# Attention and a top-1 expert layer: logits before rows in each chunk, and another order of the work behind attention

## The chip, the core and the metric

One core of a Trainium2 chip runs the whole program. Its engines are TensorE (PE, matrix products into PSUM banks), VectorE (DVE), ScalarE (ACT), GpSimd (POOL) and SyncE (SP, which here only starts transfers); each takes its instructions in the order of the program and waits at semaphores. The metric is the device time of one execution in microseconds (us), the median over several runs.

## The reference

Sliding-window attention with a distance bias, and a layer of eight experts of which each token takes one:

```python
def _attn_ref(q, k, v):                       # 8 batches, 8 heads, 576 tokens, 64 wide
    scores = scale * np.matmul(q, k.transpose(0, 1, 3, 2))
    mask = (rel >= 0) & (rel < window)        # window 128
    scores = np.where(mask, scores + bias[None], -1000000000.0)
    attn = np.exp(scores - np.max(scores, axis=-1, keepdims=True))
    attn = attn / (np.sum(attn, axis=-1, keepdims=True) + 1e-09)
    return np.matmul(attn, v)

def _moe_ref(x, w_gate, w1, w2):              # x: 4608 tokens x 512; 8 experts, 1024 wide
    logits = x @ w_gate
    expert_idx = np.argmax(logits, axis=1)
    ...
    gate_w = probs[np.arange(N), expert_idx]
    for e in range(E):
        mask = expert_idx == e
        h = np.maximum(x[mask] @ w1[e], 0.0)
        out[mask] = gate_w[mask, None] * (h @ w2[e])
```

## The kernel before, in words

**Attention** takes 36 chunks of 128 tokens in an order that is written by hand: four steps for a chunk, and the table `LAGS` says in which step each part of a chunk stands (scores L138, mask L152 and maximum L155, exponentials L159, transposes L168, products with v L196, `rows`). `rows` ends a chunk: one product (L206) turns the chunk's result and forms its gate logits, into `r_ps`; then DVE multiplies by the reciprocal row sum in two instructions, E (the 16 gate columns of each of 4 pairs of heads) and D (the 128 result columns of each pair), both at L211. `done` (L1079) sums the gate columns into logits (lg, L1085) and lets SP store the rows to memory (`xd`, L1092).

**Routing** goes by groups of chunks (`GROUPS`). `route` is a generator in stages: one-hot (oh, L413) | rank product on PE (L419 to L423), pick, gates and their store (L494), run, t | p, lp, c | eq (L456), rr (L460) | index product ip (L466) and base (L468). A stage is issued at every fourth step. In most stages the small products of PE go into spare columns of `r_ps`, the bank that `rows` has last filled. The last full group is (30, 5), chunks 30 to 34; its last three stages stand in `route_last`, which routes chunk 35 alone (one-hot l_oh L515, rank L519, four l_lp L540, index products L543, idx L545).

**Early slices.** While routing ends, PE already runs the first expert's first layer for 256 tokens that were routed long before: seven slices of 12 products of 128x256 (L634, into the banks of `s_ps`), each followed by e_hh on ACT (L636) and e_hl on DVE (L637). A slice uses the bank of the last but one, so it waits for that slice's e_hl. `EP` and `LE` set where the slices stand.

**Experts.** `moe_static` begins with the second layer of these seven slices for two tiles (L762, `y_ps`, 42 products); between them stand the transposes of the rows of the next tokens (L596), which POOL gathers from memory (L587) once idx is there and the last rows and gates are stored. Ahead of the gathers POOL clears three pairs of buffers (hh and hl, L781). From then on PE works through eight experts.

The functions that the change touches, and what calls them:

Of the kernel before, what the change touches and what calls it, by code (L numbers as in the profile page):

```python
# [22 lines left out]
QB = 32  # L23
NP = H // 2
# [12 lines left out]
def attention(ctx, tc, st, qT, kT, v, c1, cb, iw, load_c2, chunk_done, chunks, begun):  # L37
# [163 lines left out]
    def rows(ch, subs, xT, rsum):  # L201
        rinv = small.tile([128, H], F32, name="rinv")
        nc.vector.reciprocal(out=rinv, in_=rsum)
        st["r_ps"] = r_ps = ps_r.tile([128, NP, 256], F32, name="r_ps")
        for p in range(NP):
            nc.tensor.matmul(out=r_ps[:, p, 0:XW], lhsT=xT[:, p, :], rhs=iw_sb[:, p, :], start=True, stop=True)  # L206
        x_sb = xp.tile([128, NP, XW], F32, name="x_sb")
        for lo, n in ((128, E), (0, D)):
            cols = slice(lo, lo + 2 * n)
            split = lambda ap: ap[:, :, cols].rearrange("q p (c x) -> q p c x", c=2)  # L210
            nc.vector.tensor_tensor(  # L211
                out=split(x_sb), in0=split(r_ps),
                in1=rinv.rearrange("q (p c) -> q p c", c=2).unsqueeze(3).to_broadcast([128, NP, 2, n]), op=ALU.mult)
        chunk_done(ch, subs, x_sb)

    ahead = {}
    done_q, done_v, scaled = {(0, 0), (0, 1), (0, 2)}, {(0, 0), (0, 1)}, {(0, 0)}
# [75 lines left out]

# [37 lines left out]
QA = 4  # L331
KA = 16
RB = 2
LW = (0, 0, 0, 0)
FREE_T = 146
WU = (9, 1, 1, 1, 1, 1, 2, 2, 2, 2, 2, 1, 0)
PACE = {21: (122, 126, 130, 132, 134), 27: (138, 142, 144, 146, 148), 30: (149, 150)}
# [1 line left out]
EARLY = 256  # L339
LATE = 27  # L340
NE = 7
EP = {60: "z", 134: "g", 143: "p0", 146: "p1", 147: "0", 149: "1", 150: "2"}
LE = ("3", "4", "56", "")
PF = (2, 3, 4)
BY_PARTS = 2
MAXOV = N // 128 + E
# [46 lines left out]
def route(tc, st, lg, c0, G, groups):  # L393
# [29 lines left out]
        nc.tensor.matmul(out=rank[:, E * g:], lhsT=tri[:, 1, :], rhs=f2(oh[:, 0:G - g]), start=False, stop=g == G - 1)  # L423
    pick = rp.tile(sh3, F32, name="pick")
    nc.vector.tensor_tensor(out=pick, in0=rank.rearrange("p (g e) -> p g e", e=E), in1=oh, op=ALU.mult)
    gate = rp.tile([128, G], F32, name="gate")
    nc.vector.tensor_reduce(out=gate, in_=ex, axis=AX.X, op=ALU.add)
    put_gates(tc, st, gate, groups)
    new = run[:, c0 + G, :]
    nc.vector.tensor_reduce(out=new, in_=oh.rearrange("p g e -> p e g"), axis=AX.X, op=ALU.add)  # L430
    nc.vector.tensor_tensor(out=new, in0=new, in1=run[:, c0, :], op=ALU.add)
    s = st["rank"][:, c0:c0 + G]
    nc.vector.tensor_reduce(out=s, in_=pick, axis=AX.X, op=ALU.add)
    t = rp.tile([128, G], F32, name="t")
    nc.vector.tensor_scalar(out=t, in0=s, scalar1=1.0 / 128, scalar2=-63.5 / 128, op0=ALU.mult, op1=ALU.add)
    nc.vector.tensor_scalar(out=t, in0=t, scalar1=12582912.0, scalar2=-12582912.0, op0=ALU.add, op1=ALU.add)
    if c0 + G == LATE:
        cnt = rp.tile([128, E], BF16, name="s_cnt")
        nc.vector.tensor_copy(out=cnt, in_=new)
# [17 lines left out]
                            in1=c.unsqueeze(2).to_broadcast(sc3), op=ALU.is_equal)  # L457
    rr = rp.tile([128, G, 2, E * TT], BF16, name="rr")
    for k, n in enumerate(("tokh", "tokl")):
        nc.vector.tensor_tensor(out=rr[:, :, k, :], in0=eq,  # L460
                                in1=st[n][:, c0:c0 + G].unsqueeze(2).to_broadcast(sc3), op=ALU.mult)
    yield
    ip = spare(st, 1, E * TT)
# [33 lines left out]
def route_last(tc, st, lg, ch, groups):  # L497
    nc = tc.nc
    rp = st["rp"]
    run = st["run"]  # L500
    tri = st["tri"]
    prev = rp.tile([128, E], BF16, name="l_prev", bufs=1)
    nc.vector.tensor_copy(out=prev, in_=run[:, ch, :])
    mx = rp.tile([128, 2], F32, name="l_mx", bufs=1)
    nc.vector.tensor_reduce(out=mx[:, 0:1], in_=lg, axis=AX.X, op=ALU.max)
    key = rp.tile([128, E], F32, name="l_key", bufs=1)
    nc.vector.scalar_tensor_tensor(out=key, in0=lg, scalar=mx[:, 0:1], in1=st["rev"], op0=ALU.is_ge, op1=ALU.mult)
    nc.vector.tensor_scalar(out=mx[:, 1:2], in0=mx[:, 0:1], scalar1=-1.0, scalar2=None, op0=ALU.mult)
# [12 lines left out]
    for r in st["rest"]:
        next(r)
        next(r)
    st["warm"](1)
    rr = rp.tile([128, 2, E], BF16, name="l_rr", bufs=1)
    for k, n in enumerate(("tokh", "tokl")):
        nc.vector.tensor_scalar(out=rr[:, k, :], in0=oh, scalar1=st[n][:, ch:ch + 1], scalar2=None, op0=ALU.mult)
    pick = rp.tile([128, E], F32, name="l_pick", bufs=1)
    s = st["rank"][:, ch:ch + 1]
    nc.vector.tensor_tensor_reduce(out=pick, in0=rank, in1=oh, op0=ALU.mult, op1=ALU.add, scale=1.0, scalar=0.0,  # L530
                                   accum_out=s)
    put_gates(tc, st, gate, groups)
    st["warm"](2)
    for r in st["rest"]:
        list(r)
    ip = st["ps_x"].tile([128, 512], F32, name="x_ps")[:, 0:E * TT]
    t0 = EARLY // 128
    for t in range(t0, TT):
        lp = rp.tile([128, 128], BF16, name=f"l_lp{t}", bufs=1)
        nc.vector.tensor_scalar(out=lp, in0=st["i128"], scalar1=s, scalar2=-128.0 * t, op0=ALU.subtract,  # L540
                                op1=ALU.is_equal)
        for k in range(2):
            nc.tensor.matmul(out=ip[:, E * t:E * t + E], lhsT=lp, rhs=rr[:, k, :], start=(k == 0), stop=(k == 1))  # L543
# [7 lines left out]
    st["warm"](3)  # L551


def slots(tc, st, pool, e, s0):
# [123 lines left out]
def moe_static(ctx, tc, st, w12, out):  # L678
# [7 lines left out]
    yp = ctx.enter_context(tc.tile_pool(name="m_y", bufs=YB))  # L686
    ps_l = ctx.enter_context(tc.tile_pool(name="ps_l", bufs=2, space=PSUM))
    ps_e = ctx.enter_context(tc.tile_pool(name="ps_e", bufs=1, space=PSUM))
    ps_y = [ctx.enter_context(tc.tile_pool(name=f"ps_y{n}", bufs=1, space=PSUM)) for n in (0, 2)]
    xs = {}  # L690
    xg = {}
    ys = {}
# [365 lines left out]
@with_exitstack  # L1058
def attn_moe_kernel(ctx, tc, qT, kT, v, c1, cb, c2, iw, w12, out):
    nc = tc.nc  # L1060
    st = {"stages": []}
    moe_pools(ctx, tc, st)
    load_c2 = load_consts(tc, st, c2)
    moe_early(ctx, tc, st)
# [4 lines left out]
    with ExitStack() as actx:  # L1069
# [9 lines left out]
        def done(ch, subs, x_sb):  # L1079
# [4 lines left out]
            lg = lgs["lg"]  # L1084
            nc.vector.tensor_reduce(out=lg[:, g, :], in_=x_sb[:, :, 128:XW].rearrange("q p (c e) -> q e p c", c=2),  # L1085
                                    axis=AX.XY, op=ALU.add)
            for lo in (0, 2):
                if lo == 2 and subs[0][0] == subs[2][0]:
                    continue
                n = 64 if subs[0][0] != subs[2][0] else 128  # L1090
                t0 = subs[lo][0] * S + QB * subs[lo][1]
                nc.sync.dma_start(out=st["xd"][t0:t0 + n].rearrange("t (p x) -> t p x", p=NP),  # L1092
                                  in_=x_sb[QB * lo:QB * lo + n, :, 0:SUB])
# [67 lines left out]
```

## Time and profile before

| | |
|---|---|
| median of three runs | 673.66 us (673.47, 673.66, 675.84) |
| profiled execution, its own time | 674.61 us |
| its span | 672.8 us |
| mean granted TensorE clock in it | 0.996 |
| busy in the span | PE 647.7, DVE 398.6, ACT 313.1, POOL 309.2 us |

The span is the part of the profiled execution between its first and its last instruction; 1.8 us of its time lie outside. Attention takes roughly the first 235 us, the passage to the experts the stretch up to 262 us, the experts the rest. A busy share says how long an engine had work, not whether it set the time; that is read from which engine stood idle for which.

### The profile page before, as it was taken

How to read it: one execution, taken by the hardware profiler on the slowest of the kernel's cores; microseconds unless marked ns; L12 is line 12 of the kernel's file. 1: busy time of each engine (PE TensorE's matmuls, PEld its weight loads, DVE VectorE, ACT ScalarE, POOL GpSimd, SP SyncE). 2: the span in 40 equal slices, each digit the busy share in tenths (PEclk: the TensorE clock that was granted, in tenths of full speed). 3: DMA queues.
4: the chain of work that ended last, by engine and by line, in shares of the span. 5: the costliest groups of instructions: out<-in, count | busy, mean ns of one | idle time of the engine just before them, and what ended most of it. 6: DMA issues, size and time to landing. Idle time of an engine off the chain costs nothing.

```text
span 672.8 us, 15622 instructions
## 1 busy us (share of the span) xinstructions
PE 647.7 (96%) x5937; PEld 551.2 (82%) x5937; DVE 398.6 (59%) x976; ACT 313.1 (47%) x940; POOL 309.2 (46%) x425
## 2 busy tenths in 40 slices
PE   7899999999999989999999999999999999999995
PEld 3688787787787878999988988989898989888884
DVE  3468878877888777553555355365456455456411
ACT  3777778887776511442234234233434333333311
POOL 2546567786654413016524751860762560471202
PEclk8999999999999999999999999999999999999999
DMA  9477696795853316335323442532543542453201
GB/s 319 131 199 182 177 248 164 256 261 133 264 144 82 94 34 189 111 117 170 93 81 109 144 128 82 181 106 85 173 107 109 174 114 77 159 147 111 89 0 59
DMA packets 55360, 94.24 MB, mean 140 GB/s; under 512 B 11622, under 2 KB 31334, under 8 KB 54386
## 3 DMA queue, kind: packets, MB, share of 16 engines
q1 hardware_dynamic: 46882, 73.18, 37.2%
q0 software_dynamic: 8400, 20.02, 10.4%
q8 instruction: 48, 0.79, 0.5%
q14 instruction: 30, 0.25, 0.1%
HBM read 74.20 MB, written 18.97 MB: 138 GB/s over the span
## 4 chain that ended last, share of the span: by engine, by line
PE 51%; issue 8%; POOL 3%; DMA 1%; DVE 1%; ACT 1%; POOLq 0%; ACTq 0%
PE y_ps L762 24%; PE l_ps L634 23%; POOL xg L614 2%; POOL out L749 1%; PE x_ps L762 1%; PE s_ps L634 1%; PE x_ps L596 1%; DMA xd<-x_sb 1%; PE x_ps L196 1%; DMA xg<-xd,idx 0%; PE r_ps L206 0%; DMA out<-y,od_pidx 0%; DVE x_sb L211 0%; ACT pe L159 0%; POOLq L812 0%
## 5 line engine op out<-in xcount | busy, mean ns | idle before, releaser
L637 DVE SCALAR_TENSOR_TENSOR hl<-l_ps,hh 128x334 fp32r<-128x334 f32 (+7 forms) x104 | 52.7, 506 | 162.5 <-ACT hh L636 162.4
L636 ACT ACTIVATE hh<-l_ps 128x334 fp32r<-128x334 f32 (+7 forms) x104 | 46.9, 451 | 216.4 <-PE l_ps L634 216.1
L614 POOL DMA_INDIRECT xg<-xd,od_idx x112 | 114.8, 1025 | 35.8 <-issue 35.2
L159 ACT ACTIVATE pe<-s_ps,nmax 128x128 f32<-128x128 f32 x288 | 102.2, 371 | 48.9 <-DVE nmax L155 39.8
L762 PE MATMUL y_ps<-wh,hh 128*128 128x512 f32 (+2 forms) x288 | 114.2, 397 | 0.0
L762 PE MATMUL y_ps<-wl,hh 128*128 128x512 f32 (+2 forms) x288 | 113.6, 394 | 0.0
L762 PE MATMUL y_ps<-wh,hl 128*128 128x512 f32 (+2 forms) x288 | 113.5, 394 | 0.0
L749 POOL DMA_INDIRECT out<-y,od_pidx x34 | 36.3, 1068 | 153.7 <-ACT y L768 147.2
L852 DVE TENSOR_TENSOR wl<-w_raw,wh 128x512 fp32r<-128x512 f32 x114 | 73.9, 689 | 23.2 <-ACT wh L848 22.1
L634 PE MATMUL l_ps<-xh,wl 128*128 128x304 f32 (+9 forms) x416 | 80.8, 316 | 0.0
L634 PE MATMUL l_ps<-xh,wh 128*128 128x304 f32 (+9 forms) x416 | 80.7, 316 | 0.0
L634 PE MATMUL l_ps<-xl,wh 128*128 128x304 f32 (+9 forms) x416 | 80.6, 316 | 0.0
L634 PEld LDWEIGHTS l_ps<-xh,wh 128*128 128x128 f32 x416 | 68.3, 189 | 7.4
L634 PEld LDWEIGHTS l_ps<-xh,wl 128*128 128x128 f32 x416 | 66.1, 189 | 2.0
L634 PEld LDWEIGHTS l_ps<-xl,wh 128*128 128x128 f32 x416 | 66.0, 189 | 1.9
L196 PE MATMUL x_ps<-pT,v_sb 128*64 128x128 f32 (+2 forms) x1152 | 66.4, 265 | 0.1
L762 PEld LDWEIGHTS y_ps<-wh,hl 128*128 128x128 f32 (+2 forms) x288 | 53.0, 184 | 13.9
L196 PEld LDWEIGHTS x_ps<-pT,v_sb 128*64 128x64 f32 (+1 forms) x1152 | 57.0, 137 | 7.8 <-issue 2.8
L762 PEld LDWEIGHTS y_ps<-wl,hh 128*128 128x128 f32 (+2 forms) x288 | 53.1, 184 | 11.6
L762 PEld LDWEIGHTS y_ps<-wh,hh 128*128 128x128 f32 (+2 forms) x288 | 53.0, 184 | 10.8 <-ACT hh L636 0.4
L159 ACT ACTIVATION_READ_ACCUMULATOR pe<-s_ps,nmax 128x1 f32 x288 | 60.2, 209 | 0.0
L138 PE MATMUL s_ps<-k_sb,q_sb 64*64 64x192 f32 (+2 forms) x1152 | 57.3, 307 | 2.6 <-DMA k_sb<-kT 2.6
(207 smaller groups left out, 980.6 us busy)
## 6 DMA issues: line engine op xcount, KB each, us to landing
w_raw<-w SPq DMA_DIRECT2D x64, 512.0 KB, 3.7
q_sb<-qT SPq DMA_DIRECT2D x40, 256.0 KB, 7.1
xd<-x_sb SPq DMA_DIRECT2D x32, 258.0 KB, 4.9
v_sb<-v SPq DMA_DIRECT2D x32, 256.0 KB, 4.9
k_sb<-kT SPq DMA_DIRECT2D x7, 1152.0 KB, 8.3
xg<-xd,od_idx POOLq DMA_INDIRECT x112, 3.2
xd<-x_sb SPq DMA_DIRECT2D x8, 129.0 KB, 4.2
v_sb<-v SPq DMA_DIRECT2D x8, 128.0 KB, 4.7
```

What stands on the lines that cost most here:

```text
L138: nc.tensor.matmul(out=s_ps[halves(a), c, n, x0:x1], lhsT=blocks["q", b, m][h, 2 * g + n, qs], rhs=batch[b][h, 2 * g + n, k0:k0 + x1 - x0] ...
L159: nc.scalar.activation(out=pe[:, h, :], in_=s_ps[:, c, n, lo:lo + 128], func=AF.Exp, bias=nmax[:, 2 * c + n:2 * c + n + 1], scale=1.0, acc ...
L196: nc.tensor.matmul(out=x_ps[64 * c:64 * c + 64, p, q], lhsT=blocks["v", b, m - 1 + kb][0:kk, D * h:D * h + D], rhs=pT[0:kk, kb, h, q], sta ...
L596: nc.tensor.transpose(out=x_ps[:, d, :], in_=g[:, SUB * d:SUB * d + 128], identity=st["ident"])
L614: ins = tc.nc.gpsimd.indirect_dma_start(out=g[:, s], out_offset=None, in_=parts, in_offset=bass.IndirectOffsetOnAxis(ap=idx[:, s], axis=0),)
L634: nc.tensor.matmul(out=ps, lhsT=a[:, 128 * d:128 * d + 128], rhs=b[:, d], start=(k == 0), stop=(k == 11))
L636: nc.scalar.activation(out=hh, in_=ps, func=AF.Relu)
L637: nc.vector.scalar_tensor_tensor(out=hl, in0=ps, scalar=0.0, in1=hh.bitcast(F32), op0=ALU.max, op1=ALU.subtract)
L749: ins = nc.gpsimd.indirect_dma_start(**kw).ins
L762: nc.tensor.matmul(out=ys[t][0:m], lhsT=a[:, tl], rhs=b[:, 512:1024], start=(f == 0 and k == 0), stop=(f == 7 and k == 2))
L852: keep(tc, eng.tensor_tensor(out=wl[:, sl], in0=raw[:, sl], in1=wh.bitcast(F32)[:, sl], op=ALU.subtract))
```

## The change

In `rows` only E stands right behind the product now; lg follows, and D and the store of the rows are put on a list (`st["later"]`) that is emptied at the end of the step, in `route_last` behind the rank products of chunk 35. In `route`, rank and t come ahead of run and the gates. The two rr of group (30, 5) go to POOL. The second early slice stands with the first ahead of that group's rank; in `route_last` the stages p to rr of that group stand ahead of slices 3 and 4, and the four l_lp ahead of the gates. The banks of the first tiles' second layer are swapped, so that `y_ps` no longer takes a bank on which base (before L468) is read.

```diff
+        def scale(lo, n):
...
+        scale(128, E)
+        chunk_done(ch, subs, x_sb, lambda: scale(0, D))
...
+        while st["later"]:
+            st["later"].pop(0)()
         if s in EP:
             early(EP[s])
...
-LW = (0, 0, 0, 0)
+LW = (0, 0)
...
-EP = {60: "z", 134: "g", 143: "p0", 146: "p1", 147: "0", 149: "1", 150: "2"}
-LE = ("3", "4", "56", "")
+EP = {60: "z", 134: "g", 143: "p0", 146: "p1", 147: "0", 149: "12"}
+LE = ("34", "56")
...
-        nc.vector.tensor_tensor(out=rr[:, :, k, :], in0=eq,
+        eng = nc.gpsimd if c0 + G == N // 128 - 1 else nc.vector
+        eng.tensor_tensor(out=rr[:, :, k, :], in0=eq,
...
     nc.vector.tensor_scalar(out=oh, in0=key, scalar1=mk, scalar2=None, op0=ALU.is_equal)
+    for r in st["rest"]:
+        next(r)
+        next(r)
     st["warm"](0)
...
-    for r in st["rest"]:
-        next(r)
-        next(r)
-    st["warm"](1)
+    while st["later"]:
+        st["later"].pop(0)()
...
-    ps_y = [ctx.enter_context(tc.tile_pool(name=f"ps_y{n}", bufs=1, space=PSUM)) for n in (0, 2)]
+    ps_y = [ctx.enter_context(tc.tile_pool(name=f"ps_y{n}", bufs=1, space=PSUM)) for n in (2, 0)][::-1]
...
-            for lo in (0, 2):
...
+            def store():
+                scale()
+                for lo in (0, 2):
...
+            st["later"].append(store)
```

Three places show the order. First DVE at the end of one chunk in attention, before and after (E is 128x4x16, D is 128x4x128):

```order
L203 RECIPROCAL rinv<-rsum 128x8
L211 TENSOR_TENSOR x_sb<-r_ps,rinv 128x4x16
L211 TENSOR_TENSOR x_sb<-r_ps,rinv 128x4x128
L1085 TENSOR_REDUCE lg<-x_sb 128x8
L152 COPY_PREDICATED s_ps<-c_sb,s_ps 128x4x128
```

```order
L203 RECIPROCAL rinv<-rsum 128x8
L212 TENSOR_TENSOR x_sb<-r_ps,rinv 128x4x16
L1093 TENSOR_REDUCE lg<-x_sb 128x8
L212 TENSOR_TENSOR x_sb<-r_ps,rinv 128x4x128
L152 COPY_PREDICATED s_ps<-c_sb,s_ps 128x4x128
```

lg has moved ahead of D, and nothing else.

Then DVE behind attention, from the one-hot of chunk 35 on (p to rr are group (30, 5), names with l_ are chunk 35), before and after:

```order
L515 TENSOR_SCALAR l_oh<-l_key,mk 128x8
L1031 MEMSET ov_cum 128x1
L637 SCALAR_TENSOR_TENSOR e_hl<-s_ps,e_hh 128x256
L444 SCALAR_TENSOR_TENSOR p<-t,rank 128x5
L446 TENSOR_TENSOR lp<-c_sb,p 128x640
L449 TENSOR_SCALAR c<-mk 128x5
L451 TENSOR_SCALAR big<-rank 128x5
L453 TENSOR_TENSOR c<-c,t 128x5
L454 TENSOR_TENSOR c<-c,big 128x5
L456 TENSOR_TENSOR eq<-c_sb,c 128x240
L460 TENSOR_TENSOR rr<-eq,c_sb 128x5x48 x2
L637 SCALAR_TENSOR_TENSOR e_hl<-s_ps,e_hh 128x256
```

```order
L521 TENSOR_SCALAR l_oh<-l_key,mk 128x8
L449 SCALAR_TENSOR_TENSOR p<-t,rank 128x5
L1039 MEMSET ov_cum 128x1
L451 TENSOR_TENSOR lp<-c_sb,p 128x640
L454 TENSOR_SCALAR c<-mk 128x5
L456 TENSOR_SCALAR big<-rank 128x5
L458 TENSOR_TENSOR c<-c,t 128x5
L459 TENSOR_TENSOR c<-c,big 128x5
L461 TENSOR_TENSOR eq<-c_sb,c 128x240
L645 SCALAR_TENSOR_TENSOR e_hl<-s_ps,e_hh 128x256 x2
L212 TENSOR_TENSOR x_sb<-r_ps,rinv 128x4x128
L534 TENSOR_SCALAR l_rr<-l_oh,c_sb 128x8 x2
```

The e_hl of slice 3 has moved behind eq, rr has left, and D of chunk 35 has come to stand behind two e_hl.

Last PE behind attention, from the end of group (30, 5)'s rank to the rank of chunk 35, before and after (the L634 or L642 rows are early slices, 12 products each):

```order
L423 MATMUL t_ps<-oh,tri 128x8
L634 MATMUL s_ps<-e_xh,wh 128x256 x4
L634 MATMUL s_ps<-e_xh,wl 128x256 x4
L634 MATMUL s_ps<-e_xl,wh 128x256 x4
L206 MATMUL r_ps<-iw_sb,xT 128x144 x4
L634 MATMUL s_ps<-e_xh,wh 128x256 x4
L634 MATMUL s_ps<-e_xh,wl 128x256 x4
L634 MATMUL s_ps<-e_xl,wh 128x256 x4
L519 LDWEIGHTS tri
L519 MATMUL x_ps<-l_oh,tri 128x8
L520 LDWEIGHTS tri
L520 MATMUL x_ps<-l_prev,tri 128x8
```

```order
L428 MATMUL t_ps<-oh,tri 128x8
L206 MATMUL r_ps<-iw_sb,xT 128x144 x4
L642 MATMUL s_ps<-e_xh,wh 128x256 x4
L642 MATMUL s_ps<-e_xh,wl 128x256 x4
L642 MATMUL s_ps<-e_xl,wh 128x256 x4
L642 MATMUL s_ps<-e_xh,wh 128x256 x4
L642 MATMUL s_ps<-e_xh,wl 128x256 x4
L642 MATMUL s_ps<-e_xl,wh 128x256 x4
L528 LDWEIGHTS tri
L528 MATMUL x_ps<-l_oh,tri 128x8
L529 LDWEIGHTS tri
L529 MATMUL x_ps<-l_prev,tri 128x8
```

Slice 2 has gone ahead of the rank (it stood first here before), and slice 4 has come ahead of the rank of chunk 35. Further on, 23 instead of 18 products of the second layer stand ahead of the first transposes of gathered rows, and all eight L543 products stand ahead of the first `y_ps` product, where they stood between such products.

## Rows read from the trace of the kernel before

**Rows 1.** The first part of the page (busy time, share of the span and number of instructions of each engine), and from its second part the granted TensorE clock in 40 slices of 16.8 us, in tenths of full speed (9 is 0.9 or more).

```profile
PE 647.7 (96%) x5937; PEld 551.2 (82%) x5937; DVE 398.6 (59%) x976; ACT 313.1 (47%) x940; POOL 309.2 (46%) x425
...
PEclk8999999999999999999999999999999999999999
```

**Rows 2.** The view of waits for TensorE (PE), 30 to 225 us of the span (the steady part of attention): what an instruction waited for, us in total, times, longest us.

```profile
PE t_ps L168 <- ACT pT L170: 4.3, 9, 0.7
PE r_ps L466 <- DVE x_sb L211: 3.1, 4, 1.2
```

**Rows 3.** The same view for VectorE (DVE), same stretch.

```profile
DVE s_ps L152 <- PE s_ps L138: 24.0, 28, 2.0
```

**Rows 4.** The view of waits for TensorE, 234 to 256 us (the passage from attention to the expert layers), same columns.

```profile
PE y_ps L762 <- DVE base L468: 0.9, 1, 0.9
PE t_ps L419 <- DVE oh L413: 0.8, 1, 0.8
PE x_ps L519 <- DVE l_oh L515: 0.6, 1, 0.6
PE s_ps L634 <- DVE e_hl L637: 0.6, 1, 0.6
```

**Rows 5.** The view of stretches: window in us: its length, then busy us (and instructions) of PE, PE weight load, DVE, ACT, POOL, then the granted TensorE clock (1 is full), DMA share, GB/s.

```profile
8.00:10.00 2.00, 1.75 (x26) 0.74 (x30) 1.06 (x2) 0.00 (x0) 0.17 (x1) 0.74 1.03 365
10.00:12.00 2.00, 1.94 (x26) 0.84 (x22) 1.13 (x3) 1.50 (x8) 0.45 (x1) 0.50 1.09 411
...
262.00:664.00 402.00, 402.00 (x2174) 353.31 (x2174) 200.56 (x430) 136.42 (x217) 161.78 (x179) 1.00 0.38 114
```

**Rows 6.** The timeline of DVE and PE around one chunk's scaling (start us, us, engine, line, operation, out<-in, shapes, count, in brackets the idle time before it and what ended it). A row of x2 joins two instructions.

```profile
80.27 0.82 DVE L211 TENSOR_TENSOR x_sb<-r_ps,rinv 128x64 f32<-128x64 f32 x2
81.01 0.26 DVE L1085 TENSOR_REDUCE lg<-x_sb 128x8 f32<-128x64 f32 x1
81.18 0.69 DVE L152 COPY_PREDICATED s_ps<-c_sb,s_ps 128x512 f32<-128x512 uint32 x1
...
81.14 0.41 PE L466 MATMUL r_ps<-rr,lp 128*128 128x48 bf16 x10 [0.88 <-DVE x_sb L211]
```

**Rows 7.** The timeline of PE at the rank matmul of a group: the first and the last of nine places like the one of the group above.

```profile
62.85 0.18 PE L419 MATMUL r_ps<-oh,tri 128*128 128x40 bf16 x1 [0.41 <-DVE x_sb L211]
...
222.24 0.17 PE L419 MATMUL r_ps<-oh,tri 128*128 128x24 bf16 x1
```

**Rows 8.** The timeline of DVE, 238 to 246 us.

```profile
238.35 0.20 DVE L425 TENSOR_TENSOR pick<-t_ps,oh 128x40 f32<-128x40 f32 x1
...
240.29 0.42 DVE L637 SCALAR_TENSOR_TENSOR e_hl<-s_ps,e_hh 128x256 fp32r<-128x256 f32 x1 [0.39 <-ACT e_hh L636]
...
242.61 0.23 DVE L515 TENSOR_SCALAR l_oh<-l_key,mk 128x8 bf16<-128x8 f32 x1
...
243.51 0.16 DVE L444 SCALAR_TENSOR_TENSOR p<-t,rank 128x5 f32<-128x5 f32 x1
...
245.49 0.73 DVE L460 TENSOR_TENSOR rr<-eq,c_sb 128x240 bf16<-128x240 f32 x2
```

**Rows 9.** The timeline of PE, 238 to 255 us.

```profile
238.17 0.72 PE L634 MATMUL s_ps<-e_xh,wh 128*128 128x256 f32 x4
...
239.68 1.14 PE L206 MATMUL r_ps<-iw_sb,xT 128*128 128x144 f32 x8
240.56 0.74 PE L634 MATMUL s_ps<-e_xh,wh 128*128 128x256 f32 x4
...
248.16 0.42 PE L466 MATMUL t_ps<-rr,lp 128*128 128x48 bf16 x10
249.45 0.47 PE L762 MATMUL y_ps<-wh,e_hh 128*128 128x512 f32 x1 [0.87 <-DVE base L468]
...
251.17 0.40 PE L762 MATMUL y_ps<-wh,e_hl 128*128 128x512 f32 x1
...
252.55 0.39 PE L762 MATMUL y_ps<-wh,e_hl 128*128 128x512 f32 x1
...
254.67 0.66 PE L596 MATMUL x_ps<-c_sb,xg 128*128 128x128 f32 x4 [0.21 <-DMA xg<-xd,idx]
```

**Rows 10.** The timeline of SyncE (SP) at the last chunk's store of rows, and the list of DMA issues of that moment: out<-in, engine, count, KB each, median us from issue to landing.

```profile
241.76 0.54 SPq L1092 DMA_DIRECT2D xd<-x_sb  x1
...
xd<-x_sb SPq DMA_DIRECT2D x1, 258.0 KB, 4.1
...
xd<-gate SPq DMA_DIRECT2D x1, 0.5 KB, 1.4
```

**Rows 11.** The timeline of GpSimd (POOL), 245 to 252 us, and from the groups by line and shape the nearest relative of an elementwise product on POOL (count | busy us, mean ns of one | idle before).

```profile
246.27 0.35 POOL L781 MEMSET hh<- 128x306 f32 x1 [16.39 <-DVE rr L460]
...
247.78 0.35 POOL L781 MEMSET hl<- 128x306 f32 x1
251.29 0.97 POOL L587 DMA_INDIRECT xg<-xd,idx  x1 [3.17 <-DVE base L548]
...
L869 POOL TENSOR_TENSOR wl<-w_raw,wh 128x512 fp32r<-128x512 f32 x14 | 18.5, 1322 | 3.5 <-ACT wh L864 3.4
```

**Rows 12.** The waits of TensorE in 0 to 60 us, and the timeline of PE at another of its pauses.

```profile
PE s_ps L138 <- DMA k_sb<-kT: 2.6, 1, 2.6
...
19.48 0.66 PE L168 MATMUL t_ps<-c_sb,pe 128*128 128x128 f32 x4 [1.03 <-ACT pT L170]
```

More of the change, by code (lines that the diff above doesn't have):

```diff
@@ L207, in rows @@
         x_sb = xp.tile([128, NP, XW], F32, name="x_sb")
-        for lo, n in ((128, E), (0, D)):
+        def scale(lo, n):
             cols = slice(lo, lo + 2 * n)
@@ L213, in rows @@
                 in1=rinv.rearrange("q (p c) -> q p c", c=2).unsqueeze(3).to_broadcast([128, NP, 2, n]), op=ALU.mult)
-        chunk_done(ch, subs, x_sb)
+        scale(128, E)
+        chunk_done(ch, subs, x_sb, lambda: scale(0, D))
     ahead = {}
@@ L425, in route @@
     nc.vector.tensor_tensor(out=pick, in0=rank.rearrange("p (g e) -> p g e", e=E), in1=oh, op=ALU.mult)
[L426 to L431, printed above, removed]
     s = st["rank"][:, c0:c0 + G]
@@ L436, in route @@
     nc.vector.tensor_scalar(out=t, in0=t, scalar1=12582912.0, scalar2=-12582912.0, op0=ALU.add, op1=ALU.add)
+    new = run[:, c0 + G, :]
+    nc.vector.tensor_reduce(out=new, in_=oh.rearrange("p g e -> p e g"), axis=AX.X, op=ALU.add)
+    nc.vector.tensor_tensor(out=new, in0=new, in1=run[:, c0, :], op=ALU.add)
+    gate = rp.tile([128, G], F32, name="gate")
+    nc.vector.tensor_reduce(out=gate, in_=ex, axis=AX.X, op=ALU.add)
+    put_gates(tc, st, gate, groups)
     if c0 + G == LATE:
@@ L531, in route_last @@
                                    accum_out=s)
+    t0 = EARLY // 128
+    lps = {}
+    for t in range(t0, TT):
+        lps[t] = rp.tile([128, 128], BF16, name=f"l_lp{t}", bufs=1)
+        nc.vector.tensor_scalar(out=lps[t], in0=st["i128"], scalar1=s, scalar2=-128.0 * t, op0=ALU.subtract,
+                                op1=ALU.is_equal)
     put_gates(tc, st, gate, groups)
-    st["warm"](2)
+    st["warm"](1)
     for r in st["rest"]:
@@ L536, in route_last @@
     ip = st["ps_x"].tile([128, 512], F32, name="x_ps")[:, 0:E * TT]
-    t0 = EARLY // 128
     for t in range(t0, TT):
-        lp = rp.tile([128, 128], BF16, name=f"l_lp{t}", bufs=1)
-        nc.vector.tensor_scalar(out=lp, in0=st["i128"], scalar1=s, scalar2=-128.0 * t, op0=ALU.subtract,
-                                op1=ALU.is_equal)
         for k in range(2):
-            nc.tensor.matmul(out=ip[:, E * t:E * t + E], lhsT=lp, rhs=rr[:, k, :], start=(k == 0), stop=(k == 1))
+            nc.tensor.matmul(out=ip[:, E * t:E * t + E], lhsT=lps[t], rhs=rr[:, k, :], start=(k == 0), stop=(k == 1))
     v = lambda ap: ap.rearrange("p (e t) -> p t e", t=TT)
@@ L550, in route_last @@
     nc.vector.tensor_tensor(out=run[:, ch + 1, :], in0=run[:, ch, :], in1=oh, op=ALU.add)
-    st["warm"](3)
 def slots(tc, st, pool, e, s0):
@@ L1060, in attn_moe_kernel @@
     nc = tc.nc
-    st = {"stages": []}
+    st = {"stages": [], "later": []}
     moe_pools(ctx, tc, st)
@@ L1077, in begun, with done @@
                     keep(tc, nc.vector.tensor_copy(out=st["hl"][:, :, j], in_=st[n]))
-        def done(ch, subs, x_sb):
+        def done(ch, subs, x_sb, scale):
             c0, G = next((c, n) for c, n in GROUPS if c <= ch < c + n)
@@ L1086, in done @@
                                     axis=AX.XY, op=ALU.add)
-            for lo in (0, 2):
[L1088 to L1093, printed above, removed]
+            def store():
+                scale()
+                for lo in (0, 2):
+                    if lo == 2 and subs[0][0] == subs[2][0]:
+                        continue
+                    n = 64 if subs[0][0] != subs[2][0] else 128
+                    t0 = subs[lo][0] * S + QB * subs[lo][1]
+                    nc.sync.dma_start(out=st["xd"][t0:t0 + n].rearrange("t (p x) -> t p x", p=NP),
+                                      in_=x_sb[QB * lo:QB * lo + n, :, 0:SUB])
+            st["later"].append(store)
             if g == G - 1:
```

## The prediction

> **What bounds the kernel now.** The busy times come first: TensorE works for 647.7 of the 672.8 us of the span [rows 1], so a change counts only where it alters PE's 25 us of idleness. The table of stretches then shows where that is not: from 262 to 664 us PE is busy for 402.00 of 402.00 us [rows 5], so a shift of whatever stands ahead of 262 goes to the end in full, either way. What remains is attention and the passage behind it, and there the views of waits are read. In steady attention PE waits for ACT (4.3 us in nine places) and for D, the row scaling: 3.1 us in four places in front of index products [rows 2]; DVE in turn waits for PE's scores 28 times, 24.0 us in all [rows 3]. The two push each other, and a delay of the one that waits least is handed on. In the passage PE waits four times for DVE: 0.84 us for the one-hot, 0.64 for l_oh, 0.57 for e_hl and 0.87 for base, 2.9 us together [rows 4].
>
> **Attention: lg ahead of D.** The same instructions run in another order, and only D's end moves. E and D together take 0.82 us, lg 0.26, and each begins some 0.08 before the end of the last [rows 6]. Before, D ends at 80.27 + 0.82 = 81.09; with lg in between it ends 0.26 and one more handover later, about 0.29 us, and the mask behind it (L152) begins some 0.12 later. Who waits for D's end? The small products of routing, since they write into spare columns of the same bank: L466 starts at 81.14, 0.05 us after D, after 0.88 us of waiting [rows 6]. I went through the groups' rank, shift and index products in `r_ps`: in nine of twelve places PE starts 0.05 us after D in this way, from 62.85 to 222.24 [rows 7]; in the other three D is long done. Nine times 0.29 is 2.6 us. Bounds: all nine absorbed by PE's waits for ACT (4.3 us, so there is room) gives 0; nine full delays and some 0.12 at four of DVE's own stretches give 3.1. I take 2.6, since behind these places PE's rows are dense and DVE, whose chain feeds ACT, waits for PE. The later store of rows is hidden: nothing reads these rows until the gathers behind attention, except for early rows that were routed long before.
>
> **The passage: slice 2 first.** PE stood 0.84 us for the one-hot, up to the rank products, which take 0.2 and end where slice 2 begins, at 238.17: so from 237.12 to 237.96. There slice 2 now runs. A slice takes 1.51 us (238.17 to 239.68), the product for chunk 35 0.88 (239.68 to 240.56) [rows 9]. Slice 2 ends at 238.6, the rank at 238.8, r_ps of chunk 35 at 239.7, slices 3 and 4 at 242.7. The 0.84 is gone, and base is no longer waited for, since the banks are swapped: 0.87 gone.
>
> **DVE beside it.** pick stands behind e_hl of slice 2, so at about 239.3 instead of 238.35. From pick to the end of l_oh DVE took 242.84 - 238.35 = 4.5 us [rows 8]; an e_hl with its wait of 0.39 (0.7 together, up to the next start) and D of chunk 35 (0.6 of the 0.82 [rows 6]) leave this stretch, so l_oh ends at about 242.6: PE's 0.64 is gone too, since slice 4 fills it. But e_hl of slice 3, for which slice 5 waits because it takes the same bank, now stands behind p, lp, c and eq. These took from 243.51 to about 245.45, where rr follows: 1.94 us [rows 8]: they end at 244.5, e_hl at 244.85. **PE waits there for some 2.05 us**, a wait that before was 0.57 (for slice 6). Then slices 5 and 6 (3.0), ip (0.42) and eight small products (some 0.35): the first `y_ps` product starts near 248.6. Before it was 249.45 with the eight still to come, so like for like about 1.4 us are gained up to here.
>
> **rr on POOL.** No row shows this product there. POOL's nearest, 128x512 with an f32 result, takes 1.32 us [rows 11]; by width 128x240 would be 0.62, and at worst one is as long as that row. DVE took 0.73 for both [rows 8]. I take 0.75 each: eq done at 244.5, both done at 246.0, while ip comes at about 247.9. Even two of 1.32 end at 247.2, so slices 5 and 6 hide it; the cost is 0 unless slice 5 waits for less than I think.
>
> **The gather.** PE now has 23 products of the second layer ahead of the first transposes, not 18. They run 0.23 us apart (six from 251.17 to 252.55) [rows 9], so they end near 254.0, and then the gathered rows must be there. Before, the gather started at 251.29, held by idx, and PE got the rows at 254.67: 3.38 us [rows 9, 11]. Now another chain sets its start. D of chunk 35 stands behind two e_hl and ends near 245.8, and its store, which was issued at 241.76 and lands after 4.1 us [rows 10], is issued 4.0 us later. Landing: 249.9. The gates' store waits for it and takes 1.4: 251.3. POOL's memsets wait for it as well: the row at 246.27 names rr, which was long done, but 246.27 is 0.4 behind the store's landing (241.76 + 4.1). Six memsets took from 246.27 to 248.13, 1.86 us [rows 11]; from 250.35 they end at 252.2. The gather starts at 252.3, the rows are there at 255.7, and PE stands for 1.7 us in front of the transposes. Gain against before: five more products done (1.15) less a start 1.03 later: 0.1 us. Bounds: with the rows there in time, 1.15 + 0.6 = 1.8 gained (the memsets do not hold the gather and the store lands as fast as the gates' one); with D 1 us later, behind an e_hl that itself is late, 0.9 lost. I take 0.1, for each link of this chain has its row.
>
> In that chain a rule of the Trainium skill speaks otherwise than the row. The gather moved 258 KB in 3.38 us by the rows. The page "DMA: Bandwidth & Descriptors", section "Anatomy of one DMA — SWDGE (gpsimd) path", puts a transfer started by GpSimd at about 2.0 us plus its bytes over 436,000 per us, which makes 2.6 us here, an estimate by that page. By it PE would have the rows at 254.9 and the gain would be 0.9; the trace does not agree with it, and the row decides.
>
> **The sum.** The profiled execution took 674.61 us, 1.8 of them outside the span. 674.61 + 2.6 - 0.1 = 677.1. The median of the runs shown is 673.66, 0.95 lower, so the forecast in that measure is 673.66 + 2.5 = **676.2 us**, 0.4% slower. A measurement of this kernel tells about 0.5% (3.4 us) from no change, so this counts as the same.
>
> **Rivals.**
> - *The delays in attention are absorbed and the gather is in time.* For it: PE's 4.3 us of waits for ACT, which a later PE would shorten; DVE's part up to the next exponentials is only 0.12 later. Against it: PE is dense between these places. With 0 for attention and 0.1 to 1.8 gained, 673.6 to 671.9; I put it at 672.7.
> - *TensorE's clock falls in the new pauses (slower).* After PE's wait of 2.6 us for the first keys [rows 12], which ended at 8.19, the granted clock was 0.74 from 8 to 10 us and 0.50 from 10 to 12 [rows 5]: 2 x 0.26 + 2 x 0.50 = 1.5 us of work lost; full speed and half speed are 2.4 and 1.2 GHz. The change makes two pauses, 2.05 and 1.7 us, where before none in the passage was over 0.9. Against it: a pause of 1.03 us at 19.48 [rows 12] lies in a slice with a clock of 0.9 or more [rows 1], and the new ones lie between that and the one with the fall. One such fall makes 677.7, two 679.2. It decides from where a pause of about 2 us is enough.
> - *The chain through the store is longer than worked out (slower).* The rows of chunk 35 stand behind five links in series; if D or POOL is 1 us later, the passage loses 0.9 instead of gaining 0.1: 677.2.
> - *The late D does not act because PE does not wait for it.* It would show as no more waiting at L466 and L419 than before; the time is then the first rival's. It has no chance of its own.
>
> **How the numbers follow.** Forecast 0.55 (674.6 to 677.0), first rival 0.20, clock 0.15, longer chain 0.10. The range goes from 672.4, which leaves out the lower part of the first rival and a hidden gain beyond it, to 678.3, which takes in one fall of the clock but not two: about 0.1 is left out on either side. Faster by over 0.5% means below 670.3, more than any sum of the bounds gives: 0.05. Slower by over 0.5% means above 677.03: the clock (0.14 of its 0.15), most of the longer chain (0.07) and the forecast's upper edge (0.04), 0.25. That leaves 0.70 within 0.5%.
>
> **What would show it.** In the waits of PE in attention: four waits of L466's place for x_sb grow from 3.1 to about 4.3 us, and nine starts lie 0.05 us behind the second scaling. In the passage: no wait for oh, l_oh or base; one of some 2 us of an early slice for e_hl; one of 1.7 us of the transposes for xg, with the gather's start a few tenths behind six memsets that start after the last store has landed. The granted clock from 243 to 262 us settles the second rival. The prediction is wrong if PE's second layer ends ahead of 262 us by clearly more or less than the attention's delay, or if attention's end does not move.

## The result, and the profile after

The changed kernel takes 680.22 us (median of 6; 679.6 to 681.52) beside 674.62 for the one before (6 runs; 673.47 to 677.11). The ratio is 1.0079 with a 95% interval of 1.0063 to 1.0095: 5.3 us slower (4.2 to 6.4), where 2.5 were forecast, and outside the range. Its profiled execution took 680.64 us, 678.9 of them in the span. One execution in the experiments below, of e2, took 3573 us and is left out.

The first part of the page, and one stretch of the passage (window, length, busy us of PE, PE load, DVE, ACT, POOL, granted clock, DMA share, GB/s):

```profile
PE 648.2 (95%) x5937; PEld 551.0 (81%) x5937; DVE 402.0 (59%) x974; ACT 313.3 (46%) x940; POOL 311.9 (46%) x427
...
250.00:252.00 2.00, 2.00 (x17) 2.00 (x18) 1.97 (x11) 0.35 (x1) 0.76 (x2) 1.00 0.00 0
```

PE's busy time is 648.2 against 647.7 us [rows 1], and the granted clock is 1.00 in every such stretch from 238 to 274 us: no work was added, all of the loss is waiting. The waits of PE from 30 to 225 us (us in total, times, longest):

```profile
PE t_ps L168 <- ACT pT L170: 5.5, 9, 1.3
PE r_ps L472 <- DVE x_sb L212: 4.6, 5, 1.4
PE r_ps L424 <- DVE x_sb L212: 1.1, 2, 0.7
PE r_ps L482 <- DVE x_sb L212: 0.8, 1, 0.8
```

Before, beside the 3.1 us of L466 [rows 2], the same view has

```profile
PE r_ps L419 <- DVE x_sb L211: 0.4, 1, 0.4
PE r_ps L476 <- DVE x_sb L211: 0.2, 1, 0.2
```

So the small products of routing wait 6.5 us for D instead of 3.7. In the passage, 225 to 275 us:

```profile
PE s_ps L642 <- DVE e_hl L645: 3.4, 2, 2.0
PE x_ps L604 <- DMA xg<-xd,idx: 2.8, 2, 1.5
```

None of the four waits of [rows 4] is left in its place, but two new waits for e_hl and two for gathered rows have come, and each of these is longer than any of those. Their places on PE's timeline (start us, us, line, operation, tiles, idle before and its end):

```profile
237.86 1.23 PE L206 MATMUL r_ps<-iw_sb,xT 128*128 128x144 f32 x8
...
241.89 0.73 PE L642 MATMUL s_ps<-e_xh,wh 128*128 128x256 f32 x4 [1.37 <-DVE e_hl L645]
...
243.58 1.23 PE L206 MATMUL r_ps<-iw_sb,xT 128*128 128x144 f32 x8
...
249.93 0.73 PE L642 MATMUL s_ps<-e_xh,wh 128*128 128x256 f32 x4 [2.00 <-DVE e_hl L645]
...
260.31 0.66 PE L604 MATMUL x_ps<-c_sb,xg 128*128 128x128 f32 x4 [1.32 <-DMA xg<-xd,idx]
...
267.38 0.63 PE L604 MATMUL x_ps<-c_sb,xg 128*128 128x128 f32 x4 [1.47 <-DMA xg<-xd,idx]
```

The product of rows for chunk 34 starts at 237.86; before, it was 234.47. Slice 2 waits 1.37 us, slice 5 2.00, the first transposes 1.32, and the third ones another 1.47. DVE beside it:

```profile
241.42 0.42 DVE L645 SCALAR_TENSOR_TENSOR e_hl<-s_ps,e_hh 128x256 fp32r<-128x256 f32 x1
...
249.13 0.41 DVE L461 TENSOR_TENSOR eq<-c_sb,c 128x240 f32<-128x240 f32 x1
249.46 0.75 DVE L645 SCALAR_TENSOR_TENSOR e_hl<-s_ps,e_hh 128x256 fp32r<-128x256 f32 x2
250.12 0.68 DVE L212 TENSOR_TENSOR x_sb<-r_ps,rinv 128x512 f32<-128x512 f32 x1
```

POOL and SP:

```profile
249.62 1.14 POOL L466 TENSOR_TENSOR rr<-eq,c_sb 128x240 bf16<-128x240 f32 x2 [16.67 <-DVE eq L461]
254.91 0.35 POOL L789 MEMSET hh<- 128x306 f32 x1 [4.14 <-DVE od_base L1007]
...
256.89 1.00 POOL L595 DMA_INDIRECT xg<-xd,idx  x1 [0.15 <-DVE od_key L992]
...
259.50 0.98 POOL L595 DMA_INDIRECT xg<-xd,idx  x1 [0.30 <-issue]
```

```profile
250.83 0.55 SPq L1103 DMA_DIRECT2D xd<-x_sb  x1
254.53 0.33 SPq L500 DMA_DIRECT2D xd<-gate  x1
```

PE's shift against before, read at the same instruction: -1.4 us at the first product of rows (30.32 against 31.73; the start-up varies between executions, it is 29.32 in e9, the same kernel), +3.4 at chunk 34's, +3.9 at chunk 35's (243.58 against [rows 9]), +6.5 at the first layer behind the passage (268.99 against 262.51), and +6.1 at the span's end. So one part came in attention and one between 244 and 269 us.

### The profile page after: what moved, and what is told of

Read it like the earlier page. It is cut to its first block, busy times and chain, and to the rows that moved or that the text cites. A ratio compares the mean times of both kernels' runs of the same rounds, so it can differ in the third digit from the quotient of the medians.

```text
span 678.9 us, 15621 instructions
## 1 busy us (share of the span) xinstructions
PE 648.2 (95%) x5937; PEld 551.0 (81%) x5937; DVE 402.0 (59%) x974; ACT 313.3 (46%) x940; POOL 311.9 (46%) x427
## 4 chain that ended last, share of the span: by engine, by line
PE 53%; issue 8%; POOL 2%; DMA 1%; DVE 1%; POOLq 0%; ACT 0%; DVEq 0%; ACTq 0%
PE y_ps L770 26%; PE l_ps L642 24%; DMA xg<-xd,idx 1%; PE s_ps L642 1%; POOL out L757 1%; PE x_ps L770 1%; POOL xg L622 1%; PE r_ps L206 0%; PE x_ps L604 0%; POOL xg L595 0%; PE x_ps L196 0%; DVE x_sb L212 0%; POOLq L820 0%; DVE lg L1093 0%; DVE lp L451 0%
## 5 line engine op out<-in xcount | busy, mean ns | idle before, releaser
L642 PE MATMUL l_ps<-xh,wl 128*128 128x304 f32 (+9 forms) x416 | 80.7, 316 | 0.0
L642 PE MATMUL l_ps<-xh,wh 128*128 128x304 f32 (+9 forms) x416 | 80.7, 316 | 0.0
L642 PE MATMUL l_ps<-xl,wh 128*128 128x304 f32 (+9 forms) x416 | 80.6, 315 | 0.0
L642 PEld LDWEIGHTS l_ps<-xh,wh 128*128 128x128 f32 x416 | 68.2, 189 | 7.4
L642 PEld LDWEIGHTS l_ps<-xh,wl 128*128 128x128 f32 x416 | 66.1, 189 | 2.0
L642 PEld LDWEIGHTS l_ps<-xl,wh 128*128 128x128 f32 x416 | 66.0, 189 | 1.9
L856 ACT CAST wh<-w_raw 128x1024 fp32r<-128x1024 f32 x57 | 59.5, 1044 | 0.0
```

Source lines behind the costliest of these rows:

```text
L642: nc.tensor.matmul(out=ps, lhsT=a[:, 128 * d:128 * d + 128], rhs=b[:, d], start=(k == 0), stop=(k == 11))
L856: keep(tc, nc.scalar.copy(out=wh, in_=raw))
```

## The experiments

Each kernel was timed beside the kernel before on the same chip. Differences are in us against that kernel's median there (675.05 for e1 to e4, 672.88 for e5 to e8, 673.08 for e9 to e12), with the 95% interval. The changed kernel itself was timed again only with e9 to e12; where e1 to e8 are set against it, that is across such groups.

**e1, attention alone.** The kernel before, with lg ahead of D for chunks 0 to 33:

```diff
...
+        scale(128, E)
+        if ch < 34:
+            chunk_done(ch, subs, x_sb, lambda: scale(0, D))
+        else:
+            scale(0, D)
+            chunk_done(ch, subs, x_sb, lambda: None)
...
```

> The kernel before, with lg ahead of D (and the store behind D) for chunks 0 to 33 alone; the passage is as before. Theory: the later end of D costs what PE's waits for x_sb grew by in the trace of the change (3.7 to 6.5 us), so +2.8 us against before, with those waits near 6.5 us again and the passage unchanged. Rival one: the place of D does not matter and the loss is all behind attention: 0 to +0.5 us. Rival two: the whole growth of attention in that trace (4.8 us from the first chunk to the last, the 1.7 us in which VectorE stood near 219 among it) belongs to the order: +4.8 us.

Measured: +3.2 (2.0 to 4.2). PE's waits for D in attention:

```profile
PE r_ps L473 <- DVE x_sb L212: 4.6, 5, 1.4
PE r_ps L426 <- DVE x_sb L212: 1.1, 2, 0.7
PE r_ps L483 <- DVE x_sb L212: 0.5, 1, 0.5
```

They make 6.2 us, near the changed kernel's 6.5, and behind attention the waits are those of [rows 4] again. Rival one falls; 4.8 is outside the interval.

**e2, the passage alone.** The changed kernel, chunks 0 to 33 as before:

```diff
+        if ch < 34:
+            scale(0, D)
...
+            if ch < 34:
+                store()
+            else:
+                st["later"].append(store)
```

> The changed kernel, but chunks 0 to 33 scale and store as before (E, D, lg). Theory: +2.7 us against before (5.5 less 2.8), PE's waits for x_sb in attention near 3.7 us, and in the passage the same waits as in the trace of the change: some 1.4 us of slice 2 and 2.0 of slice 5 for e_hl, some 1.3 and 1.5 of two transposes for gathered rows. Rival one: +5 us, the passage alone. Rival two: 0 or faster, the passage alone is as good as before and the loss is attention's.

Measured: +1.9 (1.1 to 2.6), a little under the theory; both rivals fall. With e1 this makes 5.1, close to the 5.3 of the whole change. In the passage:

```profile
PE s_ps L644 <- DVE e_hl L647: 3.4, 2, 2.0
PE x_ps L606 <- DMA xg<-xd,idx: 1.7, 2, 1.4
```

The same two waits of slices. In this trace the clock fell behind the second, which ended at 246.97; the same happened later in e9, the changed kernel once more, behind its 1.38 us wait for rows, which ended at 258.42 (stretches of e2, then of e9):

```profile
246.00:248.00 2.00, 1.03 (x5) 1.03 (x6) 1.97 (x7) 0.00 (x0) 1.14 (x2) 0.66 0.04 0
248.00:250.00 2.00, 2.00 (x11) 2.00 (x11) 1.29 (x9) 0.06 (x1) 0.00 (x0) 0.50 0.45 128
```

```profile
260.00:262.00 2.00, 2.00 (x8) 1.57 (x8) 1.70 (x8) 0.00 (x0) 0.99 (x2) 0.61 0.97 393
262.00:264.00 2.00, 2.00 (x9) 1.65 (x8) 0.65 (x5) 0.59 (x1) 0.90 (x1) 0.54 1.00 336
```

2 x (0.34 + 0.50) = 1.7 us of PE's work are lost in e2, and 2 x (0.39 + 0.46) = 1.7 in e9: half speed, 1.2 instead of 2.4 GHz, for some 3.4 us. Five traces have the pause of 2.0 us (the changed kernel, e2, e3, e4, e9); in e2, e3 and e4 the clock fell behind it, in e9 only behind the later pause, in the changed kernel's first trace not at all.

Most of the loss is hidden. From chunk 35's product of rows to the first transposes e2, e3 and e4 take 17.04, 16.97 and 17.04 us; without the fall there it is 16.73 (changed kernel) and 16.78 (e9). A slower PE comes later to rows for which it would have waited: 0.29, 0 and 0 us instead of 1.32 and 1.38.

**e3, two banks.** Slices 1 and 2 issued by two calls:

```diff
-            early(EP[s])
+            for op in ([*EP[s]] if EP[s].isdigit() else [EP[s]]):
+                early(op)
```

> The changed kernel, but slices 1 and 2 are issued by two calls and so take two banks; the order on every engine stays. Theory: slice 2 waits 1.4 us for e_hl of slice 1 only because one call gives both the same bank; without that all that follows comes 1 to 1.4 us earlier: +4.2 us against before, and slice 2's wait is gone. Rival: the gathered rows set the end anyway and the time is given back in front of the transposes: +5.3 us as with the change.

Measured: +3.1 (2.2 to 4.0), 2.2 less than the change. The passage, and the first transposes:

```profile
PE s_ps L643 <- DVE e_hl L646: 2.0, 1, 2.0
```

```profile
258.97 0.66 PE L605 MATMUL x_ps<-c_sb,xg 128*128 128x128 f32 x4
```

Slice 2's wait is gone, slice 5's stays: all behind slice 2 comes earlier, the gathers too, and the rival falls. The theory was right on the cause and too low on the gain. The first transposes wait no longer, but that is the clock's doing: it fell behind slice 5 (0.80, 0.50 and 0.85 from 248 to 254 us), and PE came when the rows were just there, 3.35 us behind the gather's start at 255.62.

**e4, clearing behind the gathers.**

```diff
-    for x in hs:
-        for a in x:
-            nc.gpsimd.memset(a[:, min(CAPS):].bitcast(F32), 0.0)
     for f in range(NE):
...
+    for x in hs:
+        for a in x:
+            keep(tc, nc.gpsimd.memset(a[:, min(CAPS):].bitcast(F32), 0.0))
     list(order)
```

> The changed kernel, but POOL clears hh and hl behind the three first gathers instead of ahead of them. Theory: memsets hold the first gather, so it starts 0.9 us earlier, at the landing of the last gates, and the third no longer meets the weight transfers and the next gathers: the two waits for gathered rows, 2.8 us in all, fall to about 1: +3.8 us against before. Rival: the last gates' landing is what holds the gather and the clearing is free: +5.3 us.

Measured: +6.8 (5.3 to 8.2), nothing gained. The last gates' store, its landing time, and POOL:

```profile
256.67 0.33 SPq L500 DMA_DIRECT2D xd<-gate  x1
...
xd<-gate SPq DMA_DIRECT2D x1, 0.5 KB, 1.4
```

```profile
259.07 0.98 POOL L595 DMA_INDIRECT xg<-xd,idx  x1 [6.39 <-DVE runb L988]
```

The gates land at 256.67 + 1.4 = 258.07 and the gather starts 1.00 later, with no memset ahead of it (the first one starts at 262.57). The changed kernel's first trace has no landing for its store of 254.53; in e9, the same kernel, the store of 252.67 takes 1.4 too, and the gather starts at 255.03: 0.96 behind. The clearing was free; the landing of the last gates holds the gather. The theory falls, the rival holds. PE's waits for rows cannot tell here: they are gone from this trace, but the clock fell in it (0.62 and 0.52 from 252 to 256 us). What makes 6.8 out of the rival's 5.3, which is just inside the interval, stays open.

**e5, lg twice.** e1 with lg computed a second time ahead of D, to double the delay:

```diff
+            if ch < 34:
+                nc.vector.tensor_reduce(out=lg[:, g, :], ...)
             scale()
```

> The kernel before with lg ahead of D in chunks 0 to 33, and lg computed twice there, so D's end lies about 0.55 us later than before instead of 0.29. Theory: what the order costs in attention (3.2 us with one lg) grows with the delay of D's end, place by place, to 6 to 6.5 us against before, and PE's waits for x_sb grow by 2.6 us once more, to about 9 us. Rival: the loss comes from the order alone (handovers, a stretch of VectorE that stands once), or the second lg is absorbed: +3.2 to +4 us.

Measured: +7.6 (6.6 to 8.6). Waits for D:

```profile
PE r_ps L473 <- DVE x_sb L212: 6.3, 5, 1.7
...
PE r_ps L426 <- DVE x_sb L212: 2.6, 4, 1.0
```

```profile
229.15 0.17 PE L426 MATMUL r_ps<-oh,tri 128*128 128x24 bf16 x1 [1.21 <-DVE x_sb L212]
```

With L483's 0.5, as in e1, the view from 30 to 225 us makes 9.4, after 6.2 in e1 and 3.7 before. In this trace the last of the nine places lies behind 225 us; it waits 1.2 more. Together that is 6.9 more than before, for 7.6 measured: the loss follows the waits for D, and the rival, by which a second lg would be absorbed, falls. It is larger than the theory's 6 to 6.5, since two of the places at which D had long been done (0.30 and 0.24 us) and the last one now wait too. A second lg also makes all that stands behind it on DVE later; e10 and e11 separate the two.

**e6, rows of chunk 35 first.**

```diff
+    while st["later"]:
+        st["later"].pop(0)()
     for r in st["rest"]:
         next(r)
...
-    while st["later"]:
-        st["later"].pop(0)()
```

> The changed kernel, but D of chunk 35 and its store are issued right behind l_oh, ahead of p to eq. Theory: the chain rows' store, last gates' store, first gather sets when PE gets the gathered rows; the store is issued 2.5 us earlier, the gather starts with idx, some 2 us earlier, and the waits for gathered rows (2.8 us) go, while e_hl of slice 3 comes 0.6 us later and slice 5 waits 2.6 instead of 2.0: +3 to +3.5 us against before. Rival: idx or the last gates hold the gather just as long: +5.3 us or more.

Measured: +4.6 (3.6 to 5.6), against +6.9 for the changed kernel at the same level of before (e9). The first gather, which waits no longer for gates but for idx and base, and PE:

```profile
254.50 0.99 POOL L595 DMA_INDIRECT xg<-xd,idx  x1 [1.09 <-DVE base L557]
```

```profile
247.51 0.47 PE L770 MATMUL y_ps<-wh,e_hh 128*128 128x512 f32 x1 [0.49 <-DVE p L449]
...
264.40 0.63 PE L604 MATMUL x_ps<-c_sb,xg 128*128 128x128 f32 x4 [1.75 <-DVE ov_le L1046]
```

The gather starts 11.83 us after the product of rows of chunk 35 (242.67 here) instead of 13.31 (256.89 - 243.58), and the first transposes come 1.5 us earlier after that product too, with a wait of 0.38. The store chain did hold it; the gain is 2.3, though idx takes over after 1.5. But the kernel came out slower than the theory's 3 to 3.5, and two things were not expected. Ten products of the second layer (247.51 on) now stand ahead of slice 5, which therefore waits no longer: the scheduler did this, not the edit, and how the 2.3 divide between it and the gather is not shown. And the third transposes wait 1.75. The profile names a small instruction of DVE that neither writes nor reads what they need; their rows were asked for at 257.06, 7.3 us before, so they most likely wait for these.

**e7, e_hl of slice 3 first.**

```diff
-LE = ("34", "56")
+LE = ("3", "4", "56")
...
+    st["warm"](0)
     for r in st["rest"]:
         next(r)
         next(r)
-    st["warm"](0)
+    st["warm"](1)
...
```

> The changed kernel, but e_hl of slice 3 stands ahead of p to eq on VectorE. Theory: slice 5's wait of 2.0 us goes, and with it the fall of the granted clock behind it that three of the traces show; but the gather is held by the store chain, so most of it is given back as a longer wait in front of the transposes: +4 to +5 us against before. Rival: the wait is on the path in full: +3.3 us or less.

Measured: +8.1 (6.9 to 9.4). The passage:

```profile
PE x_ps L605 <- DMA xg<-xd,idx: 2.9, 2, 2.5
PE s_ps L643 <- DVE e_hl L646: 2.4, 3, 1.4
```

Slice 5 waits 0.57 instead of 2.00 (1.37 of the 2.4 are slice 2's, 0.51 slice 6's), and the transposes wait 2.9 us for rows. The rival falls: the wait was not on the path, the gathered rows were. The theory's 4 to 5 fails too: it came out no faster than the changed kernel. The scheduler also places some later work otherwise here. 2.45 of the 2.9 us stand ahead of the second transposes (264.97): their gather went out at 258.07, SP's weight transfers at 258.19, where in the changed kernel these go out at 259.63, behind the third gather. That this is what costs the time was not tried.

**e8, all four.** e2, e3, e6 and e7 in one kernel.

> The changed kernel with E, D, lg as before in chunks 0 to 33, two banks for slices 1 and 2, D of chunk 35 and its store right behind l_oh, and e_hl of slice 3 ahead of p to eq. Theory: each of the four costs of the change is taken away and what it saves in the passage stays: PE waits for neither e_hl nor gathered rows for more than 0.5 us, and the kernel is 1 to 2.5 us faster than before. Rival: the waits come back elsewhere in the passage (idx, or the transposes for rows): within 0.7 us of before.

Measured: -1.0 (-1.7 to -0.3), at the lower edge of the theory; the rival's 0.7 is inside the interval. The passage:

```profile
PE x_ps L608 <- DMA xg<-xd,idx: 0.8, 1, 0.8
PE x_ps L608 <- DVE ov_n_u L1047: 0.8, 1, 0.8
```

No wait of a slice for e_hl is left; here too second-layer products stand ahead of slices 5 and 6. The first transposes wait 0.8 us for rows, and the third another 0.8, as in e6 under the name of a small instruction of DVE, 6.6 us behind their gather's start (251.00). So the theory's limit of 0.5 us is not met.

**e9, the changed kernel again.**

> The changed kernel as it is, beside the other three. Theory: what it loses depends little on the chip: +5.3 us against before, 4 to 6.5. Rival: where VectorE does not stand once near 219 us, the delays of D are absorbed less, since no long wait follows them, and it loses 6.5 us or more.

Measured: +6.9 (5.5 to 8.1); with the first comparison's 4.2 to 6.4 the two overlap, and theory and rival cannot be told apart by the time. The trace has what the rival describes. DVE does not stand near 219 us, and the last of the nine places, which did not wait before (222.24 [rows 7]) nor in the changed kernel's first trace, does:

```profile
223.61 0.17 PE L424 MATMUL r_ps<-oh,tri 128*128 128x24 bf16 x1 [0.92 <-DVE x_sb L212]
```

The waits for D make 7.3 us here. Still attention, from the first product of rows to chunk 34's, is 3.9 us longer than before, less than the 4.8 of the first trace (206.61 and 207.54 after 202.74).

**e10 and e11, small products later.** In the kernel before, and in that of e1:

```diff
-            if k[1] <= s and (s in PACE[k[2]] if k[2] in PACE else s % 4 == 2):
+            if k[1] <= s and (s in PACE[k[2]] if k[2] in PACE else s % 4 == 3):
```

> The kernel before, but the stages of routing (all but the paced ones) are issued one step later, so half of the products with v (16, about 1.1 us of PE) stand between the product of rows and the small products of routing. Theory: these small products wait for D, 3.7 us in attention, only because they stand right behind; with 1.1 us of work between, the waits fall below 1 us in all: 2 to 3 us faster than before. Rival: other waits (scores, ACT) take their place: within 0.7 us of before.

> The kernel of e1 (lg ahead of D in chunks 0 to 33) with the same later stages. Theory: what lg ahead of D costs, it costs through the small products that wait for D, so with 1.1 us of other work ahead of them its cost falls from 3.2 to at most 0.7 us against the run above: 1.3 to 3 us faster than before. Rival: the cost comes through VectorE's own queue, whose mask starts 0.12 us later per chunk: about 3 us slower than the run above.

Measured: -2.8 (-3.7 to -1.8) and -1.1 (-2.0 to -0.3). Waits for D in e10, then in e11:

```profile
PE r_ps L466 <- DVE x_sb L211: 1.2, 1, 1.2
PE r_ps L476 <- DVE x_sb L211: 0.2, 1, 0.2
```

```profile
PE r_ps L473 <- DVE x_sb L212: 1.4, 1, 1.4
PE r_ps L426 <- DVE x_sb L212: 0.9, 1, 0.9
PE r_ps L483 <- DVE x_sb L212: 0.5, 1, 0.5
```

Of 3.7 us 1.4 are left in e10, in the paced stages, which did not move; that is more than the theory's 1, but the time is as it says. lg ahead of D now costs 1.6, half of e1's, as the waits differ by 1.4. More than the 0.7 of the theory, since the paced places still wait; but the rival's 3 us are out. What the order costs goes through the products that stand right behind it.

**e12.** e8 with the later stages.

> The kernel of e8 (the four costs of the change taken away) with the later stages. Theory: its 0.9 us and the 2 to 3 us of the later stages add up: 3 to 4 us faster than before, and as much faster than the changed kernel as that one is slower, together 8 to 10 us. Rival: the earlier end of attention is given back behind it: 1 us faster than before.

Measured: 668.62 us, -4.4 (-5.3 to -3.6): faster than both kernels (the changed one takes 679.36 beside it, 10.7 more), and a little better than the theory's 3 to 4.

## Why the prediction was wrong

- **Attention, lg ahead of D: mechanism right, a little too small.** The term was 2.6 us (nine places of 0.29, bounds 0 to 3.1); e1 measured 3.2. In e9, where DVE does not stand, the waits for D grew by 3.7 us, at just the nine places: seven by 0.24 to 0.36, near the 0.29 of the sum, L482 by 0.64 and the last one by 0.92. About half of L482's comes with rank and t ahead of run and gates (0.5 in e2, with lg behind D). At the last place E itself starts 2.76 us behind the product of rows instead of 2.22, since the mask ahead of it stands later; the sum had one delay for all places. e5, e10 and e11 confirm what carries it. The bound by which PE's waits for ACT absorb the delay did not act: they are 5.5 us in the changed kernel's first trace and 4.1 in e9, after 4.3.
- **The passage: -0.1 was forecast, e2 measured +1.9. This is the step that failed**, and it failed first at "There slice 2 now runs". It does not run there: it waits 1.37 us for e_hl of slice 1 (241.42 on DVE, behind D of chunk 34). I had taken each slice to use the bank of the last but one; but a bank is taken once for each call, and the string "12" makes one call with two slices. In `route_last` the strings are taken apart into calls, so "34" was right. The 0.84 saved at the one-hot became a loss of 0.5, and pick, l_oh, D of chunk 35 and the gather all moved with it. e3, with two calls, gives back 2.2, across the two groups of runs.
- **Slice 5's wait: right.** 2.05 predicted, 2.00 measured. e7, which takes most of it away, is no faster: it costs nothing while the rows are late. In the sum it had been a cost to the first `y_ps` product only.
- **The gather: time right, holder wrong.** With PE's waits 1.7 were expected at the first transposes and 1.32 came. The start was put behind six memsets; e4 shows that the gates' landing sets it, some 1.0 us later, which happens to be the same moment: the time came out right by luck. The step left out the third transposes: their gather, issued at 259.50, is used at 267.38, 7.9 us later, where the first took 3.42 (256.89 to 260.31). SP's two weight transfers and POOL's next gathers start within 2.6 us of it; that they share the DMA engines is argued, not tried. In e9 this wait did not come: the clock had fallen behind the first transposes, and PE came to the third ones later.
- **rr on POOL: right.** 1.14 us for both against 1.5, long done before ip at 252.88.
- **The clock rival, at 0.15:** the fall came in four of the five traces with the pause of 2.0 us, one of them the changed kernel's (e9), at 1.7 us of PE's work each against the 1.5 worked out; behind the 2.45 us of e7 it did not come. So from where a pause is enough stays open. But the rival's price was wrong: where the clock fell ahead of the first transposes, only 0.2 to 0.3 us of the 1.7 are left at them, since PE would have waited for rows there. In the first profiled execution of the changed kernel it did not come, so it cannot explain that trace's loss.

The 3.42 us of the gather are also the second case for the rule weighed in the prediction: the Trainium skill's page "DMA: Bandwidth & Descriptors", section "Anatomy of one DMA — SWDGE (gpsimd) path", makes this 2.6 us, an estimate by that page, and the trace again has 0.8 more.

## What to carry to other kernels

Work that is moved into a gap fills it only if its buffer is free there: follow where each buffer is taken, in the code of the call and not by a rule read off other calls. An instruction put ahead of another on an engine costs the delay of the other's end at each place where something stands right behind that end; the better cure is to put other work in between, as e10 did with the half of the products with v. And a wait that ends ahead of a later, longer one is worth nothing until that one's chain has been shortened: first the store, the gates and the gather, then the slices.

## What was not expected of the hardware

In the changed kernel's trace DVE stands 1.73 us in attention though the scores that it masks are done. DVE and PE:

```profile
219.91 0.70 DVE L152 COPY_PREDICATED s_ps<-c_sb,s_ps 128x512 f32<-128x512 uint32 x1 [1.73 <-remote]
...
217.47 0.82 PE L138 MATMUL s_ps<-k_sb,q_sb 64*64 64x192 f32 x16
```

The scores end at 218.29 and the mask starts at 219.91. The same comes in the traces of e1 to e4, in e2 with the order of before, where the mask follows scores that end at 215.72:

```profile
217.28 0.70 DVE L152 COPY_PREDICATED s_ps<-c_sb,s_ps 128x512 f32<-128x512 uint32 x1 [1.80 <-PE s_ps L138]
```

It came in none of the traces of before and e5 to e12, e9 with the changed kernel among them. So it does not go with the change. e1 to e4 ran on one chip and e5 to e12 on another, so whether it goes with the chip, the series or the execution is not shown, and what ends it stays open. It carries 0.9 of the 4.8 us by which attention was longer in the changed kernel's first trace (from -1.4 to +3.4): in e9, without it, 3.9 are left.
